# A gated recurrence and a highway layer: the last unit's two g halves side by side on TensorE, and the last 260 entries of a written order rearranged

## Chip, cores and metric

The kernel runs on one core of one Trainium2 chip. The metric is the device time of one execution in microseconds; lower is better. The kernel before takes 210.6 us, the median of 3 runs (210.52 to 210.73).

## What is computed

Four sequences of 6336 tokens with 256 channels (25344 tokens in all, float32). First a gated recurrence along each sequence, then a highway layer on its output:

```python
sig = 1.0 / (1.0 + np.exp(-f_logit))
f = lower_bound + (1.0 - lower_bound) * sig
i = 1.0 - f
for t in range(S):
    h = f[:, t] * h + i[:, t] * x[:, t]        # y[:, t] = h, then tokens are flattened
H = np.maximum(y @ w_h, 0.0)
T = 1.0 / (1.0 + np.exp(-(y @ w_t + b_t)))
out = T * H + (1.0 - T) * y
```

## The kernel before

The tokens are cut into 28 units: 23 of 1024 tokens, the others of 256 or 512 at both ends (units 0 and 1: 256, 2: 512, 26: 512, 27: 256). The 256 channels are two halves of 128, one half on the 128 partitions at a time. For each unit n the kernel issues small operations, each named by a letter, the unit, and a half or block after the point:

| name | engine | what it does | line |
|---|---|---|---|
| l, x | SP (DMA) | load the logits and x, 8 tokens per partition, 1024 KB for a full unit | 263 |
| u | ScalarE | u = sigmoid(-logits), half precision | 275 |
| b n.k | GpSimd | u*x of two tokens per partition (512 columns), pairs interleaved | 283 |
| i n.h | TensorE | transposes u of half h into PSUM | 289 |
| f n.h | ScalarE | the gate f from the transposed u | 300 |
| p n.h | TensorE | transposes b, two bf16 as one 4-byte word; needs every b of the unit | 309 |
| s n.h | VectorE | the recurrence as a scan over the unit's tokens, carried from the unit ahead | 326 |
| z, g n.m | TensorE | matmuls of y (both halves) with w_t and w_h, four per full unit | 343, 141 |
| t n.m | ScalarE | sigmoid of z | 356 |
| d n.m | VectorE | max(y*ncc, g) | 360 |
| E n.k, e n | GpSimd, VectorE | d*t; GpSimd takes blocks of 512 columns up to the unit's last number in `units`, VectorE the rest in one operation | 365 |
| o n.q | TensorE | back to tokens on partitions: y with a diagonal plus e with the identity, per block q of 4 tokens | 384, 385 |
| c n.q | ScalarE | copies the block from PSUM to SBUF | 394 |
| w n.q | SP (DMA) | writes it out, 512 KB | 399 |

The order of all these operations stands in the string `order`, written out as tokens such as `g27.0:1`; the number behind the colon is the buffer (slot). Each operation is recorded with `pin`, so every engine runs its operations exactly in the order of the list; across engines an operation waits for its operands and for its buffer, that is, until the last reader of the tile that had the slot before is done. PSUM has two one-bank slots (a0, a1: i and p) and three two-bank slots (b0 to b2: z, g, o). For the last unit alone (n = 27) both halves of g stand in one tile of an a slot, and so do both halves of z (`ffn`, line 330); there g27.0 and g27.1 are two matmuls of 256 columns each, and d27.0 and d27.1 read the tile's halves.

VectorE and GpSimd are kept apart in one respect: behind an e of VectorE the next b or E of GpSimd in the list gets a wait for it (`shared`). So the place of an e in the list is also a wait of GpSimd. SP issues loads and writes one after another; a write waits for its c, and what stands behind it on SP waits too.

Of the kernel before, what the change touches and what calls it, by code (L numbers as in the profile page):

```python
# [19 lines left out]
def kernel(  # L20
# [39 lines left out]
        (0, 128, 8, 15360, 'y', 4, 2048),  # L60
        (0, 128, 8, 16384, 'y', 4, 0),
        (0, 128, 8, 17408, 'y', 4, 2048),
        (0, 128, 8, 18432, 'y', 4, 256),
        (0, 128, 8, 19456, 'y', 4, 2048),
        (0, 128, 8, 20480, 'y', 4, 2048),
        (0, 128, 8, 21504, 'y', 4, 1024),
        (0, 128, 8, 22528, 'y', 4, 1024),
        (0, 128, 8, 23552, 'y', 4, 512),
        (0, 128, 4, 24576, 'y', 4, 512),
        (0, 128, 2, 25088, 'y', 4, 256),  # L70
    ]
    order = """
l0:0 l3:1 pc:1 wh u0:0 i0.0:1 i0.1:0 k*10 l1:2 x0:0 wt cc dg f0.1v:0 f0.0:1 x1:1 u3:1 u1:2 i1.0*5:0 WH b0.0v:0 l2:3
# [31 lines left out]
s18.1:1 t16.0 p18.0:0 o15.1:1 t17.0:0 b19.0 s18.0 b21.2:0 o15.0:0 c14.1:2 p19.1:1 z17.1:2 c15.1:3 e16:2 E17.1:0  # L105
b20.1:1 c15.0:0 i19.0:0 z18.1:1 b20.0 b20.3 l22:4 t17.1 b20.2 w14.0 g18.0:0 f19.0:1 z18.0:2 w14.1 p19.0:0 s19.1:3
E17.3 i20.1:1 d18.0:1 w15.1 t18.1:2 t18.0 o16.1:1 E17.0 g18.1:2 o16.0:0 b21.1 s19.0 d18.1 f20.1:2 w15.0 p20.0:1
i21.1:0 u22:1 l23:5 x22:4 z19.0:2 c16.1:1 s20.0:2 c16.0:2 f21.1:3 g19.1:1 e18:1 g19.0:0 i22.0:0 d19.0:2 i21.0:1 E17.2
t19.0:1 b21.0 f22.0:1 z19.1:2 p20.1:0 f21.0:0 b21.3 t19.1 o17.0:0 w16.1 d19.1 E19.0:2 c17.0:3 o17.1:1 p21.0:1 s20.1
b22.2:2 z20.1:0 b22.1 o18.1:2 c17.1:0 E19.3 u23:2 w16.0 b22.0 b22.3 x23:5 s21.0:0 p21.1:0 o18.0:1 i23.1:1 c18.1:1  # L110
t20.1:2 b23.0:1 l24:0 g20.0:2 E19.1 g20.1:0 s21.1 c18.0:2 d20.0:1 i22.1:0 z20.0:1 f23.1:2 p22.0:1 z21.0:2 E19.2
f22.1:0 t20.0 d20.1 w17.1 p22.1:0 t21.0:0 b23.1 s22.0:1 x24:1 g21.0:0 z21.1:2 d21.0:0 u24:0 i23.0:1 o19.0:1 o19.1:0
s22.1 b23.2 b23.3 b24.2:0 E20.0:0 f23.0:3 b24.3 t21.1 p23.0:1 c19.1:0 w18.1 l25:1 x27:0 i24.0:0 s23.0:3 c19.0:1
g22.1:2 f24.0:1 g21.1:0 z22.1:1 b24.0 d22.1:2 w17.0 i24.1:1 w18.0 d21.1 z22.0:2 E21.1:1 u25:1 t22.1:1 p23.1:0 t22.0
e20 l27:2 s23.1 x26:2 g22.0:0 b24.1 E22.3:2 d22.0 f24.1:0 E21.3 o20.0:1 E21.2 o20.1:2 p24.1:1 c20.0:3 x25:3 i25.1:0
z23.1:1 w19.0 c20.1:2 E21.0 g23.1:2 z23.0:0 b25.0:2 b25.2 f25.1:3 b25.1 p24.0:0 t23.1:2 b25.3 s24.1:2 E22.1 i25.0:1
l26:3 t23.0 E22.0 o21.1:1 g23.0:0 d23.1:1 E22.2 s24.0 f25.0:2 o21.0:2 c21.1:1 g24.1:1 d23.0 w20.0 u26:2 u27:0 p25.0:1
b26.0:1 i27.1:0 c21.0:3 z24.0:0 w19.1 d24.1:0 f27.1:0 s25.0:0 o22.1:2 w20.1 b26.1 p25.1:0 z24.1:1 t24.0:0 s25.1
o22.0:0 c22.1:0 i26.1:1 w21.1 g24.0:2 t24.1 f26.1:1 E23.0:0 z25.0:1 d24.0 w21.0 e23 e24:1 c22.0:2 i26.0:1 g25.1:0
f26.0:2 p26.1:0 o23.0:2 t25.0:1 E24.0 z25.1:1 d25.1:2 c23.0:1 E24.1 t25.1 w22.1 p26.0:1 s26.1:1 o24.0:0 s26.0 c24.0:3  # L120
b27.0:0 E23.1 g25.0:2 w22.0 i27.0:0 o24.1:1 f27.0:3 w23.0 d25.0 E25.0:2 c24.1:0 p27.1:1 p27.0:0 z26.0:0 o23.1:2
t26.0:0 s27.1:2 c23.1:2 g26.0:1 s27.0 w24.0 z27.1:0 z26.1:0 t26.1 z27.0 e25 o25.1:2 g26.1:0 d26.0:0 o25.0:1 t27.1:2
c25.1:1 w24.1 d26.1 t27.0 g27.0:1 w23.1 E26.0:1 w25.1 c25.0:3 e26 o26.0:2 g27.1 w25.0 d27.0:1 c26.0:0 d27.1 E27.0:0
e27 w26.0 o27.0:1 c27.0:2 w27.0
"""

    NU = len(units)
# [312 lines left out]
```

## Time and profile before

One profiled execution took 210.65 us; its span, from first to last instruction, is 208.9 us, so 1.8 us lie outside the span. Its mean granted TensorE clock is 0.994.

| engine | busy us | share of the span |
|---|---|---|
| TensorE (PE) | 191.4 | 92% |
| VectorE (DVE) | 194.0 | 93% |
| ScalarE (ACT) | 194.9 | 93% |
| GpSimd (POOL) | 172.8 | 83% |
| 16 DMA engines, the main queue | | 93.5% |

A busy share of a TensorE matmul counts a pipelined instruction from its start to its modelled end; a stream of 512-column matmuls that start 0.22 us apart each lasts 0.38 us in the profile. In rows and chains, DVE, ACT, POOL, PE, SP are the engines, an L and a number is the line, `out<-in` are the tiles.

| operation (whole unit's shape) | mean us of one | line |
|---|---|---|
| scan s, 128x1024 | 2.34 | 326 |
| d, 128x1024 / 512 / 256 | 1.26 / 0.74 / 0.48 | 360 |
| e on VectorE, 128x2048 / 1792 / 1536 / 1024 / 512 | 1.20 / 1.08 / 0.93 / 0.69 / 0.43 | 365 |
| E on GpSimd, 128x512 / 256 | 1.16 / 0.67 | 365 |
| b on GpSimd, 128x512 | 1.17 | 283 |
| c, 128x1024 / 512 | 1.06 / 0.59 | 394 |

The first part of each operation's record overlaps the end of the one ahead on the same engine (0.08 us on VectorE), so start to start is a little less than these.

### The profile page before, as it was taken

To read this page: it belongs to the slowest core of one execution; us is meant where nothing else is said; L and a number is where in the kernel's file an instruction comes from. 1 tells how busy PE (TensorE), PEld (TensorE's weight loads), DVE (VectorE), ACT (ScalarE), POOL (GpSimd) and SP (SyncE) were. 2 spreads that over 40 slices of the span, in tenths; PEclk is the share of its full clock that TensorE was granted. 3 is DMA by queue.
4 is the path that set the end of the run, shared out by engine and by line. 5 is a ranking of instruction groups with operands and counts; after the bars stand their busy time and mean duration, and the time that the engine had idled before them with its cause. 6 is when DMAs were issued, how large, how long until landed. Compare 5 with 4: busy or idle time off the path is not lost.

```text
span 208.9 us, 4642 instructions
## 1 busy us (share of the span) xinstructions
PE 191.4 (92%) x1800; PEld 132.5 (63%) x1827; DVE 194.0 (93%) x153; ACT 194.9 (93%) x191; POOL 172.8 (83%) x164
## 2 busy tenths in 40 slices
PE   7888787989999999999999989999999999999991
PEld 2355455577675765776665765777686757776870
DVE  0799998999999999999999999999999999999951
ACT  4769979999999999999999999999999999998991
POOL 3176989789999399998799999879799997996921
PEclk9999999999999999999999999999999999999997
DMA  6999999999999999999999999999999998755576
GB/s 229 390 423 424 413 422 420 419 410 420 416 427 399 416 399 335 398 420 393 422 385 383 427 415 417 431 412 421 415 382 336 418 416 359 295 204 201 204 311 243
DMA packets 15982, 78.69 MB, mean 377 GB/s; under 512 B 1748, under 2 KB 2264, under 8 KB 10072
## 3 DMA queue, kind: packets, MB, share of 16 engines
q1 hardware_dynamic: 15952, 78.39, 93.5%
q8 instruction: 14, 0.23, 0.4%
q14 instruction: 8, 0.07, 0.1%
q10 hardware_dynamic: 8, 0.00, 0.0%
HBM read 52.43 MB, written 25.95 MB: 375 GB/s over the span
## 4 chain that ended last, share of the span: by engine, by line
PE 51%; DVE 19%; DMA 13%; ACT 6%; issue 5%; POOL 3%; SPq 1%; POOLq 0%; DVEq 0%; ACTq 0%
DMA l<-in_f_logit_dram 13%; DVE y L326 11%; PE z L343 8%; PE g L343 8%; PE op L385 7%; PE op L384 6%; DVE d L360 6%; PE bT L309 6%; PE z L141 6%; PE uT L289 6%; PE g L141 5%; DVE e L365 2%; ACT f L300 2%; ACT u L275 2%; POOL bv L283 2%
## 5 line engine op out<-in xcount | busy, mean ns | idle before, releaser
L283 POOL TENSOR_TENSOR bv<-u,x 128x512 bf16<-128x512 f16 x96 | 109.8, 1173 | 19.7 <-DMA x<-in_x_dram 10.1
L326 DVE TENSOR_TENSOR_SCAN y<-f,y,bT 128x1024 bf16<-128x1024 f16 (+5 forms) x54 | 106.6, 1991 | 1.4 <-ACT f L300 0.6
L365 POOL TENSOR_TENSOR e<-d,t 128x512 bf16<-128x512 bf16 (+1 forms) x57 | 63.6, 1132 | 11.5 <-DVE e L365 6.0
L360 DVE SCALAR_TENSOR_TENSOR d<-y,ncc,g 128x1024 bf16<-128x1024 bf16 (+2 forms) x56 | 62.9, 1141 | 2.4 <-PE g L343 1.3
L300 ACT ACTIVATE f<-uT,ncc 128x1024 f16<-128x1024 f16 (+2 forms) x53 | 55.8, 1072 | 3.4 <-PE uT L289 2.2
L356 ACT ACTIVATE t<-z,bt 128x1024 bf16<-128x1024 f32 (+2 forms) x56 | 57.3, 1057 | 0.8 <-PE z L141 0.2
L394 ACT COPY o<-op 128x1024 f32<-128x1024 f32 (+1 forms) x50 | 50.5, 1040 | 2.7 <-PE op L385 2.1
L275 ACT ACTIVATE u<-l 128x2048 f16<-128x2048 f32 (+2 forms) x28 | 48.7, 1748 | 2.9 <-DMA l<-in_f_logit_dram 2.9
L384 PE MATMUL op<-diag,y 128*128 128x128 f16 x396 | 49.6, 219 | 2.0 <-ACT t L356 1.3
L385 PE MATMUL op<-ident_b,e 128*128 128x128 bf16 x396 | 49.4, 220 | 1.8 <-POOL e L365 1.6
L385 PEld LDWEIGHTS <-e 128*128 128x128 bf16 x396 | 44.0, 113 | 7.2 <-issue 2.9
L384 PEld LDWEIGHTS <-y 128*128 128x128 bf16 x396 | 44.2, 113 | 2.0
L343 PE MATMUL g<-y,w_sb 128*128 128x512 bf16 (+1 forms) x111 | 39.2, 368 | 1.5 <-DVE d L360 0.5
L343 PE MATMUL z<-y,w_sb 128*128 128x512 bf16 (+1 forms) x112 | 39.0, 368 | 0.9 <-DVE d L360 0.4
L309 PE MATMUL bT<-ident_f,bv 128*128 128x128 f32 x198 | 31.7, 278 | 4.3 <-ACT f L300 2.4
L289 PEld LDWEIGHTS <-u 128*128 128x128 f16 x396 | 26.0, 98 | 10.9 <-issue 3.7
L289 PE MATMUL uT<-ident_h,u 128*128 128x128 f16 x396 | 30.4, 219 | 2.2 <-DVE y L326 1.7
L141 PE MATMUL z<-y,w_sb 128*128 128x512 bf16 x84 | 31.8, 379 | 0.0
L343 PEld LDWEIGHTS <-w_sb 128*128 128x128 f16 x224 | 21.7, 98 | 15.9 <-issue 0.4
L309 PEld LDWEIGHTS bT<-ident_f,bv 128*128 128x128 f32 x198 | 22.4, 141 | 13.4 <-POOL bv L283 3.1
L141 PEld LDWEIGHTS <-w_sb 128*128 128x128 f16 x184 | 17.9, 97 | 17.6 <-issue 3.0
L141 PE MATMUL g<-y,w_sb 128*128 128x512 bf16 x75 | 28.4, 379 | 0.0
(41 smaller groups left out, 51.5 us busy)
## 6 DMA issues: line engine op xcount, KB each, us to landing
out_dram<-o SPq DMA_DIRECT2D x48, 512.0 KB, 6.8
l<-in_f_logit_dram SPq DMA_DIRECT2D x23, 1024.0 KB, 10.8
x<-in_x_dram SPq DMA_DIRECT2D x23, 1024.0 KB, 10.7
l<-in_f_logit_dram SPq DMA_DIRECT2D x2, 512.0 KB, 7.4
x<-in_x_dram SPq DMA_DIRECT2D x2, 512.0 KB, 8.5
l<-in_f_logit_dram SPq DMA_DIRECT2D x3, 256.0 KB, 4.1
x<-in_x_dram SPq DMA_DIRECT2D x3, 256.0 KB, 5.6
out_dram<-o SPq DMA_DIRECT2D x3, 256.0 KB, 5.2
```

What stands on the lines that cost most here:

```text
L141: return pe.add_instruction(mybir.InstMatmult(name=nc.get_next_instruction_name(), start_tensor_calc=start, stop_tensor_calc=stop, tile_si ...
L283: shared(pin(e.tensor_mul(st[n]["bv"][:, k].rearrange("p d j -> p j d"), st[n]["u"][:, q:q + 2], st[n]["x"][:, q:q + 2])), not eng)
L289: pin(nc.tensor.transpose(uT[:, j * P:(j + 1) * P], st[n]["u"][:, j, h * P:(h + 1) * P], ident_h))
L300: pin(nc.scalar.activation(to, of, AF.Identity, scale=ncc[:, h:h + 1], bias=1.0))
L309: pin(nc.tensor.transpose(words[:, k:k + g * (P - 1) + 1:g], pair, ident_f))
L326: pin(nc.vector.tensor_tensor_scan(y[:, c:e], st[n]["f", h][:, c:e], st[n]["bT", h][:, c:e], 0.0 if fresh else carry[h], op0=ALU.mult, op1 ...
L343: pin(nc.tensor.matmul(p[:, a:e], w, half(n, "y", ki)[:, a:e], start=ki == 0, stop=ki == NH - 1))
L356: pin(nc.scalar.activation(half(n, "t", m), st[n]["z", m][:, :tokens(n)], AF.Sigmoid, bias=bt[:, m:m + 1]))
L360: pin(nc.vector.scalar_tensor_tensor(half(n, "d", m), half(n, "y", m), ncc[:, m:m + 1], st[n]["g", m][:, :tokens(n)], op0=ALU.mult, op1=AL ...
L365: shared(pin(eng.tensor_mul(st[n]["e"][:, a:e], st[n]["d"][:, a:e], st[n]["t"][:, a:e])), eng is nc.gpsimd)
L384: pin(nc.tensor.matmul(o, half(n, "y", h)[:, cols], diag[:, h], start=True, stop=False))
L385: pin(nc.tensor.matmul(o, half(n, "e", h)[:, cols], ident_b, start=False, stop=True))
```

## The change

Three entries of `units` get another share for GpSimd (units 20, 21 and 27: 256, 2048, 256 become 1024, 1024, 0), and the list from unit 19's operations to the end is in another order, with other slots. At the very end g27.1 follows g27.0 directly, ahead of o26.0, instead of behind it; e27 covers all 512 columns and there is no E27.0; d27.1 comes before d27.0; t27.0 stands behind c25.0 instead of ahead of it. e21 is new on VectorE, for E21.2 and E21.3. Nothing else of the program is changed.

```diff
-        (0, 128, 8, 18432, 'y', 4, 256),
-        (0, 128, 8, 19456, 'y', 4, 2048),
+        (0, 128, 8, 18432, 'y', 4, 1024),
+        (0, 128, 8, 19456, 'y', 4, 1024),
...
-        (0, 128, 2, 25088, 'y', 4, 256),
+        (0, 128, 2, 25088, 'y', 4, 0),
...
-i21.1:0 u22:1 l23:5 x22:4 z19.0:2 c16.1:1 s20.0:2 c16.0:2 f21.1:3 g19.1:1 e18:1 g19.0:0 i22.0:0 d19.0:2 i21.0:1 E17.2
-t19.0:1 b21.0 f22.0:1 z19.1:2 p20.1:0 f21.0:0 b21.3 t19.1 o17.0:0 w16.1 d19.1 E19.0:2 c17.0:3 o17.1:1 p21.0:1 s20.1
-b22.2:2 z20.1:0 b22.1 o18.1:2 c17.1:0 E19.3 u23:2 w16.0 b22.0 b22.3 x23:5 s21.0:0 p21.1:0 o18.0:1 i23.1:1 c18.1:1
-t20.1:2 b23.0:1 l24:0 g20.0:2 E19.1 g20.1:0 s21.1 c18.0:2 d20.0:1 i22.1:0 z20.0:1 f23.1:2 p22.0:1 z21.0:2 E19.2
-f22.1:0 t20.0 d20.1 w17.1 p22.1:0 t21.0:0 b23.1 s22.0:1 x24:1 g21.0:0 z21.1:2 d21.0:0 u24:0 i23.0:1 o19.0:1 o19.1:0
-s22.1 b23.2 b23.3 b24.2:0 E20.0:0 f23.0:3 b24.3 t21.1 p23.0:1 c19.1:0 w18.1 l25:1 x27:0 i24.0:0 s23.0:3 c19.0:1
-g22.1:2 f24.0:1 g21.1:0 z22.1:1 b24.0 d22.1:2 w17.0 i24.1:1 w18.0 d21.1 z22.0:2 E21.1:1 u25:1 t22.1:1 p23.1:0 t22.0
-e20 l27:2 s23.1 x26:2 g22.0:0 b24.1 E22.3:2 d22.0 f24.1:0 E21.3 o20.0:1 E21.2 o20.1:2 p24.1:1 c20.0:3 x25:3 i25.1:0
-z23.1:1 w19.0 c20.1:2 E21.0 g23.1:2 z23.0:0 b25.0:2 b25.2 f25.1:3 b25.1 p24.0:0 t23.1:2 b25.3 s24.1:2 E22.1 i25.0:1
-l26:3 t23.0 E22.0 o21.1:1 g23.0:0 d23.1:1 E22.2 s24.0 f25.0:2 o21.0:2 c21.1:1 g24.1:1 d23.0 w20.0 u26:2 u27:0 p25.0:1
-b26.0:1 i27.1:0 c21.0:3 z24.0:0 w19.1 d24.1:0 f27.1:0 s25.0:0 o22.1:2 w20.1 b26.1 p25.1:0 z24.1:1 t24.0:0 s25.1
-o22.0:0 c22.1:0 i26.1:1 w21.1 g24.0:2 t24.1 f26.1:1 E23.0:0 z25.0:1 d24.0 w21.0 e23 e24:1 c22.0:2 i26.0:1 g25.1:0
-f26.0:2 p26.1:0 o23.0:2 t25.0:1 E24.0 z25.1:1 d25.1:2 c23.0:1 E24.1 t25.1 w22.1 p26.0:1 s26.1:1 o24.0:0 s26.0 c24.0:3
-b27.0:0 E23.1 g25.0:2 w22.0 i27.0:0 o24.1:1 f27.0:3 w23.0 d25.0 E25.0:2 c24.1:0 p27.1:1 p27.0:0 z26.0:0 o23.1:2
-t26.0:0 s27.1:2 c23.1:2 g26.0:1 s27.0 w24.0 z27.1:0 z26.1:0 t26.1 z27.0 e25 o25.1:2 g26.1:0 d26.0:0 o25.0:1 t27.1:2
-c25.1:1 w24.1 d26.1 t27.0 g27.0:1 w23.1 E26.0:1 w25.1 c25.0:3 e26 o26.0:2 g27.1 w25.0 d27.0:1 c26.0:0 d27.1 E27.0:0
-e27 w26.0 o27.0:1 c27.0:2 w27.0
+i21.1:0 c16.1:1 z19.0:1 c16.0:2 E17.2 f21.1:3 x22:4 g19.1:0 b21.0 u22:1 b21.3 s20.0:2 z19.1:2 p20.1:0 i22.0:1 d19.1:2
+s20.1 l23:5 t19.0:1 g19.0:0 o17.0:1 i21.0:0 f22.0:1 w16.1 t19.1 e18:1 g20.1:2 c17.0:3 f21.0:0 w16.0 d19.0 p21.0:1
+o17.1:1 b22.1:2 b22.3 E19.1:2 d20.1:0 u23:2 p21.1:0 E19.2 z20.0:0 s21.0:0 o18.0:2 c17.1:0 t20.0:0 b22.0 z20.1:1
+i23.1:1 x23:5 s21.1 b22.2 g20.0:0 c18.0:1 t20.1 o18.1:2 f23.1:2 d20.0 l24:0 p22.0:0 c18.1:2 w17.0 s22.0:1 i22.1:1
+g21.0:1 z21.1:0 f22.1:0 i23.0:1 u24:0 b23.2:1 b23.1 p22.1:0 z21.0:2 d21.0:1 t21.1:2 E19.3 s22.1 g21.1:1 b23.0 E19.0
+w17.1 o19.0:0 t21.0 E20.1:0 w18.0 f23.0:3 b23.3 x24:1 d21.1 c19.0:3 l25:1 o19.1:2 p23.0:1 i24.0:0 w18.1 z22.0:1 e20
+c19.1:0 s23.0:3 b24.0:0 f24.0:1 g22.1:0 g22.0:2 E20.0 i24.1:1 x25:0 d22.1:2 b24.2 t22.0:1 p23.1:0 o20.1:1 d22.0 u25:1
+b24.1 z22.1:0 b24.3 w19.0 s23.1 f24.1:0 w19.1 E21.0:1 l26:2 e21 o20.0:2 b25.0:2 l27:3 c20.1:1 p24.1:1 t22.1 b25.1
+g23.1:1 c20.0:2 s24.1:2 i25.0:0 b25.3 z23.0:0 f25.0:3 z23.1:2 E21.1 i25.1:0 w20.1 b25.2 p24.0:1 t23.0:0 g23.0:0 t23.1
+d23.1:0 o21.0:2 E22.0:2 w20.0 o21.1:1 E22.2 f25.1:2 c21.0:3 s24.0 E22.1 p25.0:0 x27:2 d23.0 c21.1:0 z24.0:2 x26:3
+E22.3 z24.1:1 u26:2 s25.0:0 g24.1:0 p25.1:1 t24.0:2 d24.1:1 s25.1 t24.1 i26.0:0 f26.0:0 o22.0:2 o22.1:1 E23.0:0
+g24.0:0 i26.1:0 b26.1:1 c22.0:1 b26.0 c22.1:2 d24.0 u27:0 z25.0:2 i27.0:1 e23 e24:1 g25.0:1 f26.1:1 z25.1:0 d25.0:2
+w21.0 t25.0:1 E24.0 p26.1:0 o23.0:2 f27.0:3 E24.1 p26.0:1 o24.0:1 t25.1 w22.0 g25.1:0 c23.0:3 w21.1 b27.0:0 s26.1:1
+w22.1 i27.1:0 c24.0:1 o24.1:2 s26.0 p27.0:1 f27.1:2 d25.1 w23.0 p27.1:0 E23.1 z26.1:1 s27.0:2 w24.0 E25.0:2 c24.1:0
+o23.1:0 z26.0:2 s27.1 t26.1:2 c23.1:2 z27.1:1 z27.0 e25 g26.0:1 w24.1 d26.0:1 t26.0 o25.1:0 w23.1 E26.0:1 t27.1:0
+g26.1:2 d26.1 c25.1:3 o25.0:1 w25.1 c25.0:1 g27.0:0 g27.1 e26 w25.0 d27.1:0 t27.0 o26.0:0 d27.0 c26.0:0 e27:0 o27.0:1
+w26.0 c27.0:2 w27.0
```

## The prediction

> **What bounds the kernel now.** I read four views in this order: busy time by stage, the waits, the chain at the end, the DMA packets of the last 4 us. First the stages (columns: busy us and count of TensorE, its weight loads, VectorE, ScalarE, GpSimd; granted clock; DMA share; GB/s):
>
> ```profile
> 147.00:160.00 13.00, 12.87 (x130) 8.99 (x130) 13.00 (x11) 13.00 (x14) 11.84 (x12) 1.00 0.98 368
> 160.00:170.00 10.00, 9.94 (x93) 6.88 (x93) 9.72 (x6) 10.00 (x11) 10.00 (x10) 1.00 1.01 411
> 170.00:180.00 10.00, 9.93 (x90) 6.74 (x90) 10.00 (x8) 9.99 (x10) 8.71 (x9) 1.00 0.95 386
> 180.00:190.00 10.00, 9.89 (x106) 7.30 (x105) 9.98 (x7) 9.66 (x12) 10.00 (x10) 1.00 0.54 213
> 190.00:199.20 9.20, 9.15 (x99) 6.90 (x99) 9.20 (x11) 7.96 (x11) 6.39 (x6) 1.00 0.52 204
> 199.20:205.00 5.80, 4.26 (x62) 3.65 (x62) 3.05 (x6) 4.41 (x6) 1.83 (x2) 1.00 0.80 318
> ```
>
> From the place where the two lists part (147 us) to 199.2 us VectorE is full, TensorE nearly so, at full clock: no reordering can take much out of that stretch. From 199.2 on every engine has holes: there order counts. Which waits end those holes:
>
> ```profile
> DVE d L360 <- PE g L343: 1.3, 1, 1.3
> DVE d L360 <- PE op L385: 1.0, 1, 1.0
> ```
>
> And the chain that ended last (start, length):
>
> ```profile
> 200.75 0.76 DVE d L360
> 201.60 0.44 DVE e L365
> 202.08 0.25 PE op L385
> ...
> 203.00 0.23 PE g L343 x2
> 203.32 0.49 DVE d L360
> 203.85 0.07 issue
> 203.92 0.70 POOLq L435
> 204.67 0.23 PE op L385
> ...
> 205.35 0.58 ACT o L394
> ```
>
> The reader is to see that e26 ends at 202.03, that o26.0 waits for it (202.08), that g27.1 stands behind o26.0 on TensorE (203.00), and that d27.0 waits until 203.32 although g27.0, its own half, was computed at 201.44. Then E27.0 on GpSimd, o27.0, c27.0, and the last write. Last the packets (slices of 0.1 us from 205.0):
>
> ```profile
> GB/s 328 369 492 369 410 369 492 451 328 369 532 328 123 0 0 0 0 61 348 348 348 410 348 451 266 41 0 0 0 0 0 0 0 0 0 0 0 0 0 0
> ```
>
> w26.0 moves until 206.3, then 0.4 us of nothing, then w27.0 from 206.65 to 207.6. The span ends at 208.9. So the last write is not held up today, but it has only 0.4 us of room in front of it.
>
> **Part 1, the tail, counted from T, the start of o25.1** (T = 199.22 before). Before, from the timeline: g26.1 T+0.89, d26.1 T+1.53, e26 T+2.38 to T+2.80, o26.0's first e operand T+2.86, c26.0 T+3.86, d27.0 T+4.10, E27.0 T+4.73, o27.0's first e T+5.45, c27.0 T+6.13 to T+6.72, last packet T+8.40.
> After, on TensorE: o25.1, g26.1, o25.0 stand as they did, so all up to e26 keeps its distance from T. g27.0 and g27.1 run at T+2.22 to T+2.65 (two of 0.22 us issue each). What they push back is o26.0's first matmul, from T+2.43 to T+2.65; it waits for e26 until T+2.86 anyway, so this costs nothing; without that cover it would cost 0.22. On VectorE d27.1 follows e26 directly (T+2.75, successors start 0.08 before the end of the one ahead), d27.0 at T+3.15, done T+3.63 (0.48 each). What is late next: t27.0, which ScalarE now runs after c25.0 instead of ahead of it. c25.0 starts at T+2.46 as o25.0 allows, t27.0 at T+3.40 to T+3.87 (0.48). So e27 starts at T+3.97, 0.24 after its d. It is now the whole 512 columns on VectorE: 0.42 by the row of e26, the same shape; E27.0 (0.67 on GpSimd) is gone. o27.0's first e at T+4.45, c27.0 0.68 later as today: T+5.13 to T+5.72. That is **1.0 us earlier**. c26.0 waits for t27.0 and o26.0, both T+3.87: not moved.
> The writes give part of it back. w26.0 keeps its packets, T+5.8 to T+7.1. w27.0 could start 0.65 after its issue (T+6.4), but the 0.26 MB stand behind w26.0. From T+7.1 they take 0.95 us as today (T+8.05) or 0.65 at the 410 GB/s of w26.0 (T+7.75). I take T+7.95, nearer to its own row: **0.45 us** of the 1.0 is left. The Trainium skill (DMA: Bandwidth & Descriptors, "Two DMAs through the same engine are not ordered") says that descriptors of one queue on one DMA engine start in order but are pipelined, which speaks for a write that queues and against the full 1.0; the before trace shows the order, w26.0 then w27.0, but no case of the two overlapping.
>
> **Part 2, from 147 us to T.** I set the operations of each engine one behind another without gaps, in both lists, from the same starts (VectorE s20.0 146.96, TensorE z19.0 147.09, ScalarE 144.89; GpSimd's E17.2 before 150.54, after 149.42 as it no longer waits for e18). Steps are start to start in the trace: scan of 1024 2.26, d 1.18, f and t 1.0, u 1.8, c 0.9, b and E 1.13, and on TensorE i 0.45, p 0.44, z and g 0.86, o 0.89. An operation's lead is how long its operand is ready before its turn (0.1 to 0.3 us of hand-over taken off). Engines then fall behind where a lead is negative. For the kernel before this tells VectorE's three gaps rightly: at s22.0 (lead 0.51, TensorE 0.85 late, so 0.3; 0.22 read), s23.0 (0.53, TensorE 1.0 and VectorE 0.28 late, so 0.2; 0.23), d24.1 (0.1; 0.09): 0.56 in all, TensorE 1.9.
> Work added: e20 has 1024 columns instead of 1792 (0.60 for 1.0), e21 is new with 1024 (0.60), so VectorE +0.20; GpSimd gets two E20 of 1.13 for one of 0.64, two E21 instead of four, no E27.0: 1.3 less. Other operations only move.
> After, TensorE falls behind thus: 0.5 at i21.0 (its bank is free after s20.1); 1.2 at i22.1 (bank free after f23.1; ScalarE is 0.58 late since c16.0 now precedes u22 and o16.0 is not done before 146.3); 1.5 at p23.0, which waits for b23.3 (GpSimd idles 1.1 as b22.1 waits for e18); 1.65 at z24.1 (after c21.1). VectorE's smallest leads are s22.0 0.96 (TensorE then 0.75 late), s23.0 1.45 (1.5), s24.0 1.46 (1.5), d24.1 1.50 (1.65), d25.1 1.58, s27.0 1.65: it falls behind by 0.16 instead of 0.56. So e25, due at 197.82, ends at 197.82+0.16+0.93 = 198.91, and TensorE reaches o25.1 at 197.31+1.65 = 198.96. T = 199.0. The sums missed by up to 0.1 a step; VectorE at 0.56 again gives T = 199.4. I take 199.1: **0.1 us**.
> DMA moved: on SP x24 goes behind w17.0, w17.1, w18.0, so behind c18.0: issued near 160.2 instead of 156.0, behind 1.6 MB of writes. At 410 GB/s: landed 166.5; with the 8.5 of its own row 168.7. b24.0 wants it at 169.4 (after e20, which it now waits for). x25 moves from 164.6 to 163, wanted at 177. x22 is issued ahead of l23, both in time. No other load gets near its use.
>
> **Sum.** 0.45+0.1 = 0.55 off. The profiled execution took 210.65 with a span of 208.9, 1.8 outside it; 210.65-0.55 = **210.1**. The median of the three runs is 210.6, 0.05 below, which I leave inside the rounding.
>
> **Rivals.**
> (a) *The room is eaten*: T is 199.4 and w27.0 takes its 0.95, so 0.35-0.18 = 0.17 off: 210.4. For it: VectorE gets 0.20 more work, and it is the full engine. Against it: its leads are now about double where it stalled. Chance 0.22.
> (b) *Slower, by x24*: half of the 1024 KB loads of the profile take over 10.7 us from issue, x25 took 11.2. Landing at L after 169.4, x24 holds b24.0 to b24.3 (done at 175.1 if in time), and p24.1, first in its place in TensorE's list at 174.2, waits for all four: TensorE is then 1.0+(L-169.4) late for good, and T = 197.31+1.0+(L-169.4). Below L = 170.1 other waits are longer; from 171.2 the kernel is slower than before by over 0.42; at 171.4 (11.2 after issue) T = 200.3, 1.2 more than I take: 211.3. Against it: the long loads stood behind more bytes than x24 will. The same chain starts if GpSimd is late at p23.0 for another reason, where nothing is left of its lead. Chance 0.20.
> (c) *More comes off*: T 198.8 and w27.0 at the full rate: 0.42+0.65 = 1.07: 209.6. Needs every lead to hold. Chance 0.10.
> (d) *The wait stays*: d27.1 waits for something besides g27, as d27.0 does today for the later half. The order of both programs shows g27's four matmuls together, and d27.1 with waits for TensorE and GpSimd alone, where GpSimd's is long past. If it came behind o26.0 nonetheless, only E27.0's share goes: about 210.4. Within (a)'s range; 0.03.
>
> **How the numbers follow.** Forecast 0.45, 209.8 to 210.3 of its own (both ends of the write, T 199.0 to 199.2). With (a), (c) and part of (b) the range is 209.5 to 211.0. About 0.2%, 0.42 us, is what a measurement of this kernel can tell from no change. The forecast's 0.55 lies just beyond, so a fifth of its chance goes to "same". Faster: 0.36+0.10, and 0.11 from the better ends of (a) and (d) = 0.57; same: the fifth of 0.09 and the rest of (a) and (d), 0.14, = 0.23; slower 0.20.
>
> **What would show it.** Right: d27.1 starts within 0.1 us of e26's end, no GpSimd after E26.0, c27.0 at T+5.1, w27.0's packets without a gap behind w26.0's, VectorE's idle between 147 and 199 us under 0.4. Wrong: a gap before b24.0 put down to x24; VectorE waiting at s23.0 or s24.1; T after 199.4; the last packet still 8.4 us behind T.

## The result and the profile after

The changed kernel takes **210.33 us**, the median of 22 runs (210.11 to 210.71), against 210.69 for the kernel before in 22 runs on the same chips. The ratio is 0.9982 with an interval of 0.9976 to 0.9988: 0.18% or 0.38 us less, a sure gain, but just inside the 0.2% that the prediction called no change. The forecast was 0.55 us. Single executions of some kernels took 1 to 3 us longer, which makes a few intervals below wide and pulls the ratio of run 8 up (by its medians 0.45 us are off); the profiles of runs 4 and 8 are of such executions, with the time lost ahead of s20.0.

The profiled execution of the changed kernel took 210.59 us, 0.26 above its own median. It has that from far ahead of the change: s20.0, VectorE's first operation in the part that differs, starts at 147.27 instead of 146.96, since one load of x landed late (128.39 instead of 126.88). So two distances are compared below, not clock times: from s20.0 to T, the start of o25.1, and from T to the last DMA packet.

The stages, with the columns of those shown before:

```profile
147.00:160.00 13.00, 12.56 (x121) 8.60 (x119) 13.00 (x11) 13.00 (x13) 11.57 (x11) 1.00 0.98 407
160.00:170.00 10.00, 9.92 (x103) 7.21 (x102) 10.00 (x8) 10.00 (x10) 9.14 (x10) 1.00 0.94 337
...
190.00:199.20 9.20, 9.20 (x100) 6.83 (x99) 9.20 (x10) 8.41 (x11) 6.75 (x6) 1.00 0.77 306
199.20:205.00 5.80, 4.55 (x64) 3.81 (x62) 3.24 (x7) 5.07 (x8) 1.17 (x1) 1.00 0.81 319
```

VectorE shows no idle time from 147 to 199 us any more (10.00 of 10 in the second row, where it had 9.72). The waits from 147 us on, in us, times, longest; no row of that view names a DMA:

```profile
POOL e L365 <- DVE d L360: 2.4, 1, 2.4
...
DVE d L360 <- PE g L343: 0.9, 2, 0.5
```

Before, VectorE had two waits in this view: 1.0 us for g26.1, and 1.3 us for g27.1, which stood behind o26.0. Now 0.9 us in two pieces is all that the view shows, ahead of d26.0 and d26.1 (0.4 and 0.5); ahead of d27.1 only 0.13 us are left. The chain at the end (start, length):

```profile
201.74 0.44 PE g L343 x4
...
203.18 0.04 ACT t L356
203.22 0.04 issue
203.26 0.44 DVE e L365
...
204.39 0.59 ACT o L394
```

Four matmuls of g stand together at 201.74, and c27.0 runs at T+5.03 instead of T+6.13. So much for the engines; the writes, in slices of 0.1 us from 205.0 (T+5.64):

```profile
GB/s 41 492 410 328 451 369 451 410 287 492 492 328 410 369 287 410 369 348 430 389 307 62 21 20 21 0 0 0 0 0 0 0 0 0 0 0 0 0 0 0
```

Before there was a hole of 0.4 us between w26.0 and w27.0; it is gone. But the row doesn't end at once: behind the last full slice come four of 62 to 20 GB/s. 20 is about a sixteenth of the rate ahead of them, as one DMA engine of 16 still at work would give; the packets of the trace don't name their engine, so this is a reading of the rate. The last packet ends at T+8.15.

### The profile page after: what moved, and what is told of

It reads as the page before. It is cut to its first block, busy times and chain, and to the rows that moved or that the text cites. A ratio compares the mean times of both kernels' runs of the same rounds, so it can differ in the third digit from the quotient of the medians.

```text
span 208.8 us, 4668 instructions
## 1 busy us (share of the span) xinstructions
PE 192.3 (92%) x1827; PEld 132.6 (64%) x1827; DVE 194.4 (93%) x154; ACT 195.0 (93%) x191; POOL 171.7 (82%) x162
## 4 chain that ended last, share of the span: by engine, by line
PE 44%; DMA 17%; DVE 15%; ACT 12%; issue 5%; POOL 3%; SPq 2%; ACTq 0%; DVEq 0%; POOLq 0%
DMA l<-in_f_logit_dram 13%; DVE y L326 9%; PE op L385 6%; PE z L343 6%; PE op L384 6%; PE g L343 6%; PE z L141 5%; PE bT L309 5%; PE uT L289 5%; PE g L141 5%; DVE d L360 4%; ACT f L300 4%; DMA x<-in_x_dram 4%; ACT o L394 3%; ACT u L275 2%
## 5 line engine op out<-in xcount | busy, mean ns | idle before, releaser
L365 POOL TENSOR_TENSOR e<-d,t 128x512 bf16<-128x512 bf16 (+1 forms) x55 | 62.5, 1159 | 7.6 <-DVE e L365 4.5
L300 ACT ACTIVATE f<-uT,ncc 128x1024 f16<-128x1024 f16 (+2 forms) x53 | 56.4, 1073 | 3.0 <-PE uT L289 2.9
L141 PE MATMUL g<-y,w_sb 128*128 128x512 bf16 x92 | 34.9, 379 | 0.0
L141 PE MATMUL z<-y,w_sb 128*128 128x512 bf16 x92 | 34.9, 379 | 0.0
```

Source lines behind the costliest of these rows:

```text
L141: return pe.add_instruction(mybir.InstMatmult(name=nc.get_next_instruction_name(), start_tensor_calc=start, stop_tensor_calc=stop, tile_si ...
L300: pin(nc.scalar.activation(to, of, AF.Identity, scale=ncc[:, h:h + 1], bias=1.0))
L365: shared(pin(eng.tensor_mul(st[n]["e"][:, a:e], st[n]["d"][:, a:e], st[n]["t"][:, a:e])), eng is nc.gpsimd)
```

## The experiments

All on one scale: the distance from s20.0 to T, the last packet from T, and what the two together come to against the kernel before (52.26 and 8.40), beside the timed ratio and what it makes of 210.7 us.

| kernel | s20.0 to T | last packet | sum off, us | ratio (interval) | timed off, us |
|---|---|---|---|---|---|
| changed kernel | 52.09 | T+8.15 | 0.42 | 0.9982 (0.9976 to 0.9988) | 0.38 |
| 1 g27 together, in the old list | 52.30 | T+7.87 | 0.49 | 0.9973 (0.9963 to 0.9984) | 0.57 |
| 2 the new tail, in the old list | 52.28 | T+8.16 | 0.22 | 0.9988 (0.9979 to 0.9997) | 0.25 |
| 3 new list, g27 apart | 52.15 | T+8.47 | 0.04 | 0.9997 (0.9988 to 1.0006) | 0.06 |
| 4 before, without w26.0 | 52.29 | T+8.40 | -0.03 | 1.0000 (0.9968 to 1.0033) | 0.0 |
| 5 after, without w26.0 | 52.14 | T+7.30 | 1.22 | 0.9949 (0.9931 to 0.9967) | 1.07 |
| 6 t27.0 ahead of c25.0 | 52.15 | T+8.22 | 0.29 | 0.9982 (0.9973 to 0.9991) | 0.38 |
| 7 spare GpSimd product | 52.12 | T+8.14 | 0.40 | 0.9984 (0.9951 to 1.0017) | 0.34 |
| 8 E27.0 back | 52.09 | T+8.15 | 0.42 | 0.9992 (0.9970 to 1.0015) | 0.17 |
| 9 one more ScalarE instruction | 52.15 | T+8.16 | 0.35 | 0.9978 (0.9969 to 0.9986) | 0.46 |
| 10 two more | 52.14 | T+7.88 | 0.64 | 0.9969 (0.9958 to 0.9981) | 0.65 |
| 11 w25.1 in halves | 52.15 | T+8.04 | 0.47 | 0.9970 (0.9958 to 0.9982) | 0.63 |
| 12 halves and two more | 52.14 | T+7.87 | 0.65 | 0.9961 (0.9948 to 0.9975) | 0.82 |

In every row the sum of the two distances of one profile lies within the interval of the timed ratio. Runs 5 and 10 to 12 have five or six executions each, the others ten or more.

**1 to 3: the parts of the change.** First the named change alone, in the old list:

```diff
-c25.1:1 w24.1 d26.1 t27.0 g27.0:1 w23.1 E26.0:1 w25.1 c25.0:3 e26 o26.0:2 g27.1 w25.0 d27.0:1 c26.0:0 d27.1 E27.0:0
+c25.1:1 w24.1 d26.1 t27.0 g27.0:1 g27.1 w23.1 E26.0:1 w25.1 c25.0:3 e26 o26.0:2 w25.0 d27.0:1 c26.0:0 d27.1 E27.0:0
```

> The kernel before with one move: g27.1 directly behind g27.0; the list ahead of it, E27.0 on GpSimd and t27.0 stay as before. T is the start of o25.1. Theory A (the last write limits what the tail can give, the rest of the gain comes from the rearranged list ahead of T): d27.0 at T+2.75 instead of T+4.10, E27.0 at T+3.4 to 4.1, c27.0 right behind c26.0 at T+4.8 instead of T+6.1, last packet at T+8.15 instead of T+8.40: 0.25 us off, ratio near 0.9988. Theory B (the move gives all): 0.36 off or more, 0.998. Theory C (the rearranged list gives all, the end is hidden behind the writes): no change, 1.000.

Measured 210.13 us: by the median more off than the whole change, though the two intervals overlap. c27.0 comes at T+4.95, about as said, but the last packet at T+7.87, where theory A had T+8.15. Then the old list with the whole new tail (unit 27 without GpSimd's share, d27.1 first, t27.0 behind e26):

```diff
-        (0, 128, 2, 25088, 'y', 4, 256),
+        (0, 128, 2, 25088, 'y', 4, 0),
...
-c25.1:1 w24.1 d26.1 t27.0 g27.0:1 w23.1 E26.0:1 w25.1 c25.0:3 e26 o26.0:2 g27.1 w25.0 d27.0:1 c26.0:0 d27.1 E27.0:0
-e27 w26.0 o27.0:1 c27.0:2 w27.0
+c25.1:1 w24.1 d26.1 g27.0:1 g27.1 w23.1 E26.0:1 w25.1 c25.0:3 e26 t27.0 o26.0:2 w25.0 d27.1:1 c26.0:0 d27.0 e27:0
+w26.0 o27.0:1 c27.0:2 w27.0
```

> The kernel before with the whole new tail: g27.1 behind g27.0, e27 over all 512 columns on VectorE and no E27.0, d27.1 ahead of d27.0, t27.0 behind c25.0; the list ahead of it as before. Theory A: as the move alone, 0.25 off (0.9988), since c27.0 then comes at T+5.1 but the last write stands behind w26.0 in both. Theory B: all of the gain, 0.36 (0.998). Theory C: none.

Measured 210.41 us, 0.25 off as theory A said; the last packet is at T+8.16. c27.0 comes at T+5.29 only, since c25.0 starts late (T+2.74 instead of T+2.46) and pushes t27.0 and e27 back. Third, the changed kernel with g27.1 put back behind o26.0:

```diff
-g26.1:2 d26.1 c25.1:3 o25.0:1 w25.1 c25.0:1 g27.0:0 g27.1 e26 w25.0 d27.1:0 t27.0 o26.0:0 d27.0 c26.0:0 e27:0 o27.0:1
+g26.1:2 d26.1 c25.1:3 o25.0:1 w25.1 c25.0:1 g27.0:0 e26 w25.0 t27.0 o26.0:0 g27.1 d27.1:0 d27.0 c26.0:0 e27:0 o27.0:1
```

> The changed kernel with g27.1 put back behind o26.0 (t27.0 then stands ahead of c26.0 as in the changed kernel, e27 stays whole on VectorE). Theory A: the rearranged list keeps its 0.1 to 0.2, the tail is lost and e27 costs 0.1 more than E27.0 with half an e27 did: c27.0 at T+6.2, ratio against the kernel before 0.9992 to 1.000. Theory B: slower than before by up to 0.1 (1.0005). Theory C: the gain stays, 0.998.

Measured 210.57 us, and its chain has the old wait again (both d only at 203.22, c27.0 at T+6.20):

```profile
203.22 0.88 DVE d L360 x2
...
204.19 0.44 DVE e L365
...
205.32 0.59 ACT o L394
```

So the four matmuls together carry the gain: 0.53 us at the end of the old list, 0.32 at the end of the new. The rest of the tail's rewriting brings c27.0 no further (T+4.95 in 1, T+5.29 in 2, T+5.03 in the changed kernel), and something in it costs 0.3 us of the last packet. The rearranged list ahead of the tail gives 0.11 to 0.17.

**4 and 5: is it the writes?** Both kernels without the write w26.0; 512 KB of the output are left out. The edit of 5 (in 4 the same token goes from the old list):

```diff
-w26.0 c27.0:2 w27.0
+c27.0:2 w27.0
```

> The kernel before without the write w26.0: unit 26's 512 KB of output are left out, its computation is not. Theory A (before, the last write waits for its own c27.0, not for w26.0): last packet still at T+8.4, ratio 1.000 within 0.0005. Rival (the writes share the DMA engines and the end is bound by their bytes in both kernels): up to 1 us off, 0.995.

> The changed kernel without the write w26.0 (the same 512 KB left out). Theory A (in the changed kernel w27.0 stands behind w26.0): w27.0's packets start 0.65 after its issue at T+5.6 and end at T+7.2, 0.9 earlier than in the changed kernel: 1.3 us off against the kernel before, 0.994. Rival (the chain through c27.0 sets the end there too, as it does before): like the changed kernel, 0.998.

Before: nothing, the last packet stays at T+8.40. After: 0.85 us earlier, T+7.30. So w26.0 cost the kernel before nothing, and the new tail ends later because of it; T+7.30 is what c27.0 and w27.0 give without it. The row of 5 (from 203.0, slices of 0.1375 us) has a hole where w26.0 was, and no trailing slices:

```profile
GB/s 387 357 417 268 417 417 357 477 417 387 357 477 298 30 0 30 30 0 15 313 417 357 417 343 45 0 0 0 0 0 0 0 0 0 0 0 0 0 0 0
```

**6: t27.0.** A step of the prediction had e27 wait for t27.0. Here t27.0 stands ahead of c25.0 again:

```diff
-g26.1:2 d26.1 c25.1:3 o25.0:1 w25.1 c25.0:1 g27.0:0 g27.1 e26 w25.0 d27.1:0 t27.0 o26.0:0 d27.0 c26.0:0 e27:0 o27.0:1
+g26.1:2 d26.1 c25.1:3 o25.0:1 w25.1 t27.0 c25.0:1 g27.0:0 g27.1 e26 w25.0 d27.1:0 o26.0:0 d27.0 c26.0:0 e27:0 o27.0:1
```

> The changed kernel with t27.0 ahead of c25.0 on ScalarE, so that e27 no longer waits for it: e27 and c27.0 0.2 us earlier (T+3.75 and T+4.9). Theory A (w27.0 stands behind w26.0's packets): nothing comes of it, the ratio against the kernel before is the changed kernel's 0.998 within 0.0003. Rival (the chain through e27 and c27.0 still sets the end): another 0.2 off, 0.997.

e27 starts at T+3.90 with t27.0 at T+2.05 as with it at T+3.38. In the changed kernel t27.0 ends at T+3.85 and d27.0 at T+3.79, and the chain shown above names t27.0 as what released e27; take t27.0 away and d27.0 releases it at the same time. Nothing gained.

**7 to 10: what costs 0.3 us among the writes.** Between 1 and the changed kernel the writes differ in one thing. A single packet of 8 KB of another queue, q14, which the profile calls instruction, runs at T+2.12 in 1 and in a hole of the writes at T+2.13 before, but at T+4.59 in the changed kernel, in the middle of them; it takes 309 ns there. The changed kernel from 203.0 to 208.5:

```profile
GB/s 417 417 387 357 298 417 447 387 357 447 357 387 447 447 119 387 387 387 477 298 387 477 417 387 328 373 357 417 372 283 45 15 15 0 0 0 0 0 0 0
...
q14 instruction: 1, 0.01, 0.4%
```

From there the writes land late: w25.0 at T+6.75 instead of T+6.19 in 1, w26.0 at T+7.93 instead of T+7.63. By the trailing slices it is one engine of 16 that is behind. The profiles agree: where the packet runs at T+4.6 (the changed kernel, 2, 3 and 5 to 9), w25.0 lands at T+6.69 to T+6.75; where it runs at T+2.1 to T+2.5 (before, 1, 4, 10, 12), at T+6.14 to T+6.20; in 11, with the packet at T+4.21, at T+6.43. What places the packet? One theory was that it comes with GpSimd's missing E27.0. Run 7 adds a spare product of 256 columns on GpSimd in its place, run 8 gives unit 27 its share of 256 back:

```diff
+        if n == NU - 1:
+            spare = sb([P, 256], BF16, "spare")
+            pin(nc.gpsimd.tensor_mul(spare, st[n]["d"][:, :256], st[n]["t"][:, :256]))
```

```diff
-        (0, 128, 2, 25088, 'y', 4, 0),
+        (0, 128, 2, 25088, 'y', 4, 256),
...
-g26.1:2 d26.1 c25.1:3 o25.0:1 w25.1 c25.0:1 g27.0:0 g27.1 e26 w25.0 d27.1:0 t27.0 o26.0:0 d27.0 c26.0:0 e27:0 o27.0:1
+g26.1:2 d26.1 c25.1:3 o25.0:1 w25.1 c25.0:1 g27.0:0 g27.1 e26 w25.0 d27.0:0 t27.0 o26.0:0 d27.1 c26.0:0 E27.0:0 e27 o27.0:1
```

> The changed kernel, all of its list kept, with one more GpSimd operation at the place where E27.0 stood: the same product of 256 columns, written to a spare tile that nobody reads; e27 stays whole on VectorE. So far the kernels without E27.0 had an 8 KB packet of an instruction queue between the last writes, at T+4.6, and one DMA engine late from there (w25.0 landed at T+6.7 instead of T+6.2, last packet at T+8.15 instead of T+7.87); those with E27.0 had that packet at T+2.1, where no write was moving. Theory F (the packet's place costs the 0.28): with the spare operation it is back at T+2.1, last packet at T+7.9, ratio against the kernel before 0.9970. Theory G (E27.0's half of the product is what helps, the packet is harmless): as the changed kernel, 0.9982.

> The changed kernel with unit 27 as before: E27.0 on GpSimd over 256 columns, e27 over the other 256, d27.0 ahead of d27.1; all else of the new list kept, g27.1 directly behind g27.0. Theory F: the gain of the rearranged list (0.17 by T) and the whole of the tail (0.5) add up: 0.7 off, ratio 0.9967, last packet at T+7.87. Rival (the list ahead of T gives nothing, its 0.1 to 0.2 is scatter): as with g27.1 alone moved, 0.9973.

The packet stays at T+4.58 and T+4.60: that theory falls. Run 8 tells one thing more: with E27.0 back c27.0 is 0.39 us later (T+5.42), and the last packet is at T+8.15 all the same. The next theory was ScalarE's own instructions: one, then two more activations at the very start of the program. The edit of 10 (in 9 it is `range(2)`):

```diff
-    nc.scalar.activation(warm, warm, AF.Sigmoid)
+    for _ in range(3):
+        nc.scalar.activation(warm, warm, AF.Sigmoid)
```

> The changed kernel with one more instruction on ScalarE at the very start (the small warm-up activation twice, 0.26 us while ScalarE waits for its first load); the list and every tile as in the changed kernel. Reading of the runs so far: ScalarE shows a stall of 0.3 us at its 318th or 319th instruction, at T+1.2 in the kernel before and with g27.1 moved alone, at T+2.5 in all the others, and the 8 KB packet follows at T+2.1 or T+4.6. Theory H (the packet holds ScalarE's next instructions; asked for at T+2.5 it queues behind w25.1 and then delays one DMA engine among the last writes): one instruction more asks one instruction earlier, at T+1.2, the packet comes at T+2.1 and the last packet at T+7.87 instead of T+8.15: 0.28 better than the changed kernel, ratio 0.9968. Rival (the packet's place is tied to something else in the new list, or costs nothing): as the changed kernel, 0.9982.

> As the run with one more ScalarE instruction, with two. Theory H: the packet is asked for at c25.1 (T+1.1) and comes at T+2.1 or earlier; same as with one, 0.9968, unless the stall holds c25.1 by up to 0.3, then 0.998. Rival: 0.9982.

One more leaves packet and end where they were (T+4.58 and T+8.16), against theory H's forecast. With two more the packet runs at T+2.46, where few writes move, and the last packet of the writes ends at T+7.88. The engines' tail is the changed kernel's to 0.01 us (c26.0 T+3.85, c27.0 T+5.03), and s20.0 to T is the same as in 9, so it is the packet's place that counts, and not what the engines do. Run 10 from 201.0 on, with the packet, and from 205.0 on (slices of 0.1 us), where only one trailing slice is left:

```profile
GB/s 328 410 41 41 123 0 41 41 0 0 410 287 451 451 328 451 451 369 369 410 492 369 369 328 328 410 369 451 410 328 492 451 369 410 369 451 123 287 328 451
...
q14 instruction: 1, 0.01, 0.5%
```

```profile
GB/s 451 328 410 328 492 451 369 410 451 369 267 308 389 369 471 389 348 185 21 0 0 0 0 0 0 0 0 0 0 0 0 0 0 0 0 0 0 0 0 0
```

Its median, 210.02 us, is below that of both kernels, with the changed kernel's own list. It is of six executions, two of them at 210.3 and 210.4, and its interval overlaps the changed kernel's; the last packet is the firmer evidence.

**11 and 12: can more come off?** c25.1 and w25.1 in two halves, so that the writes start half a copy earlier; in 12 with the two activations of 10 besides.

```diff
-            pin(nc.scalar.copy(o[:, :j1 - j0], st[n]["op", q][:, :j1 - j0]))
+            for k in ((0, 2), (2, 4)) if (n, q) == (25, 1) else ((0, j1 - j0),):
+                pin(nc.scalar.copy(o[:, k[0]:k[1]], st[n]["op", q][:, k[0]:k[1]]))
...
-        pin(nc.sync.dma_start(rows(out, n, j0, j1), st[n]["o", q][:, :j1 - j0]))
+        for k in ((0, 2), (2, 4)) if (n, q) == (25, 1) else ((0, j1 - j0),):
+            pin(nc.sync.dma_start(rows(out, n, j0, j1)[:, k[0]:k[1]], st[n]["o", q][:, k[0]:k[1]]))
```

> The changed kernel with c25.1 and w25.1 in two halves of 2 tokens per partition each (half a block is copied as soon as its 8 matmuls are done, and its 256 KB written). Theory A (the last writes go through one queue without a gap from w25.1 on, so the first of them sets the last): the first half's packets start near T+2.1 instead of T+2.9; the last packet comes 0.4 earlier or more, T+7.7, bounded below by w27.0's own chain at T+7.3: ratio 0.9965. The ScalarE copy in two costs 0.1 to 0.2 more of ScalarE, which delays c25.0 by as much. Rival (the chain through c27.0 sets the end): 0.998 or a little worse. By theory H the added ScalarE instruction also moves the packet back to T+2.1.

> The new kernel with the first of the last three eviction copies and its write in two halves, and with two more warm-up activations on ScalarE at the very start, so that the 8 KB packet of ScalarE's instructions should move as it did in the run with two more activations (asked for at about T+1.2 to 1.5, served at about T+2.1 to 2.5, ahead of most writes; T is the start of o25.1). Theory, that the last writes are bound by the DMA engines and the packet costs 0.28 us among them: the writes now start earlier by half a copy and run without a gap from about T+2.4, so that the last packet comes at T+7.4 to 7.6, bounded below by T+7.3, which is the chain through c27.0 and w27.0 alone; 0.3 to 0.45 us better than the run with two more activations, a ratio of 0.995 to 0.9955 to the kernel before. Rival, that the split only shifts the first write and its packets still end behind the same last engine, or that the packet stays in the burst: no gain over either edit alone, the last packet at T+7.9 to 8.0, a ratio near 0.997.

Alone it gains 0.11 at the last packet, with the instruction packet still among the writes (T+4.21, not at T+2.1 as theory H had it). On top of 10 it gains nothing: T+7.87 for T+7.88. The ratio of 12 lies nearer to the theory's than to the rival's, but its interval holds both, and the last packet decides against the theory. Run 12 from 201.0 on suggests why:

```profile
GB/s 410 328 1 41 41 82 82 348 348 348 328 389 492 369 348 389 389 430 348 410 205 82 41 21 328 328 492 451 328 451 369 410 410 369 451 492 328 41 287 369
```

The halves start earlier and end earlier, and then the engines nearly stand still from 203.0 to 203.4, until w25.0 comes; and at 204.7, T+5.6, there is a dip to 41 GB/s, as in run 10 (123 at 204.6, T+5.6). There w26.0 starts, as in the changed kernel (41 in the slice at T+5.6): its c26.0 starts at T+3.85 and the write is issued at T+4.89. So the burst that ends these two kernels begins at T+5.6 with w26.0, and from there w26.0 and w27.0, 0.79 MB, take 2.3 us. That what lies ahead of it doesn't count, save an engine that is late, is a reading of these rows; no run starts w26.0 earlier.

## Why the prediction was nearly right

The direction and the mechanism held, and the range held the time. What failed is one term's size, "From T+7.1 they take 0.95 us as today (T+8.05) or 0.65 at the 410 GB/s of w26.0 (T+7.75). I take T+7.95", that is, **the 0.45 us of the tail, which measured 0.25** (8.40 less 8.15). The step counted only the bytes of the writes. Their ends came 0.28 us later by one 8 KB packet of instructions among them; with that packet ahead of them (runs 1 and 10) the last packet is at T+7.87 and T+7.88, 0.53 off, within the two ends that the step gave. That the sum came as near as it did is in part luck: the list ahead of T gave 0.07 more than was taken for it.

- *The engines in the tail* came as worked out: g27.0 and g27.1 at T+2.22 and T+2.43, o26.0 at T+2.65 at no cost, c26.0 at T+3.85, e27 at T+3.90 (3.97 was said), c27.0 at T+5.03 (5.13). d27.1 starts at T+2.92 instead of 2.75, as g27.1's matmuls end at T+2.81 only, and d27.0 is 0.16 late with it. t27.0 came as forecast (T+3.38), but it is not alone in being late next: d27.0 by then ends at nearly the same time (run 6).
- *w27.0 behind w26.0 without a gap* came as said, and that w26.0 would limit the gain is shown by 4 and 5. The Trainium skill (DMA: Bandwidth & Descriptors, "Two DMAs through the same engine are not ordered") has descriptors of one queue on one engine start in order; the trace agrees, since w27.0, issued at T+5.64 and able to end at T+7.30 alone, ends at T+8.15 behind w26.0.
- *T 0.1 earlier*: 0.17 by the profile. The gaps between VectorE's operations from s20.0 to e25, counted over the usual overlap of 0.08, come to 0.56 us before and to 0.11 in this profile (0.16 was forecast; the other profiles of the new list have 0.16 to 0.31). The two at s22.0 and s23.0 are gone. e25 ends 0.17 earlier, so the work added is nearer 0.28 than 0.20.
- *Rival (b), x24*: it landed at 167.4, and b24.0 ran at 170.0 behind e20; no wait for a DMA. *Rival (c)*: 209.6 wasn't reached by any kernel with all its work; run 12's 209.89 is the lowest. *Rival (d)* is refuted: d27.1 starts at T+2.92, with o26.0 still running until T+3.72. *Rival (a)* has the time (0.17 off, which is 210.5 from the 210.65 of the sum and 210.4 from the median), but not the reason: T was early, and the room was eaten by something that wasn't on its list.
- Sum: 0.25 + 0.17 = 0.42 off, timed 0.38.

That the rest of the change, beside the four matmuls and 0.1 to 0.2 ahead of T, is worth nothing at the last packet is shown by 2, 6 and 8. That it moves the instruction packet is shown too; that it does so by the mere number of ScalarE's instructions is likely, and stands in the last section.

## What to carry to other kernels

A reader of one half of a PSUM tile waited here for the other half's matmuls, so the matmuls that fill a shared tile belong together; that one move was worth 0.53 us at the end. When a chain that ends on a write gets shorter, look for the write in front of it and for when that one is issued: here 1.1 us off the chain became 0.53 at the last packet. And for the last two microseconds look at the other queues too: an instruction packet that falls among the last writes took half of that gain back.

## What the runs showed of the hardware

- **Instruction packets share the DMA engines with the data.** One of 8 KB took 309 ns and delayed the end of the last writes by 0.27 us (run 10 against the changed kernel). The Trainium skill (DMA: Bandwidth & Descriptors, "Queues, rings and completion order") has each engine go round between its queue rows packet by packet, with row 14 for traffic of the runtime's own, refills among it; the q14 row of the profile and the trailing slices agree with that.
- **ScalarE stumbles at a fixed place of its stream.** The semaphore instruction behind a copy mostly starts 0.02 to 0.06 us after the copy. In every one of the 14 profiles, one ScalarE instruction near the end comes some 0.3 us later than that or than its operands allow, and always at the same count: the 319th recorded one before and in runs 1 and 4, the 320th in all others. Where it falls at c25.1 (T+1.46) the 8 KB packet follows at T+2.1 to 2.5, where it falls at c25.0 (T+2.75) at T+4.2 to 4.6. One activation more (run 9) moves the late instruction from the wait behind c25.0 to c25.0 itself, two more (run 10) to the wait behind c25.1. So the packet seems to be asked for by count, and a few instructions more or fewer ahead decide on which side of a 1.3 us wait the request falls. The link between the stumble and the packet is inferred from this agreement; why the request at c25.0 is served 1.5 to 1.9 us later, and why the count is 319 in three kernels and 320 in the rest, stays open.
